# Two queued steps of the second query group, and one copy, are put at other places in the start-up order of a fused attention and feed-forward kernel

## The chip, the core and the metric

The kernel runs on one core of a Trainium2 chip. The time is device microseconds for one launch; a lower time is better. The core has a matrix engine (TensorE, PE in the profile), three others that compute on tiles (VectorE = DVE, ScalarE = ACT, GpSimd = POOL) and a queue engine (SyncE = SP). Each engine works through its own list of instructions in order, and waits on semaphores for the others. PE's weight loads have a row of their own, PEld.

## The reference

Inputs are q, k and v of shape 4 x 4 x 1088 x 32 (batch, heads, rows, head dimension), two sketches S1 and S2 of 8 x 32, and two weight matrices, w_in (128 x 2048) and w_out (2048 x 128). What is computed:

```
phi(x)[i*8+j] = (S1 x)[i] * (S2 x)[j]           for q and for k: 64 features
kv  = sum over rows of phi(k) v^T               64 x 32 per head
z   = sum over rows of phi(k)                   64 per head
att = (phi(q) kv) / (phi(q) z + 1e-6)           32 per row and head
x   = att, the four heads side by side          4352 x 128
h   = x w_in ;  g = h - tanh(h) ;  out = g w_out
```

## The kernel before, in words

The 4352 rows of x are cut into 11 groups of columns (`GROUPS`); group 0 has 256 columns, group 1 has 448, group 2 has 384. For each group g the work goes through these steps, named by the tags in the code:

- `qT{g}` (L643, DVE): the queries, loaded from memory into `qraw`, are transposed into `qT`. For batch 0 the queries come in three loads: group 0's 8 blocks, group 1's 14 blocks, and the rest.
- `p{g}` (L665, PE): the projections of the queries by the sketches, into two banks of `ps`. Those of group 1 lie in banks 4 and 5.
- `qq{g}` (L694, DVE) transposes them back, `au{g}` (L697, DVE) and `dn{g}` (L700, DVE) make the parts of the denominator, `ds{g}` (L710, PE, for groups 0, 1 and 4) adds the two halves, `rd{g}` (L723, DVE) takes the reciprocal, `an{g}` (L727, DVE) scales by it.
- `qp{g}` (L739, one half on POOL, one on DVE for groups 0 and 1) forms the products, `qpT{g}` (L746, DVE) transposes them. `qpT01` is the second half of group 0's.
- `w{g}` (L681, PE) multiplies by the sums of the keys (`ndw`); `x{g}` copies the result to `xT` in bf16. For group 0 there are two copies: `x0` on ACT and `x0b` on DVE (both L755).
- `h{g}_{jb}` (L845, PE) is one 128-row tile of x w_in, `t{g}_{jb}` (L848, ACT) its tanh, and L858 (PE) the product with w_out, 16 tiles to a group. h uses three banks in turn, so h tile n waits for the tanh of tile n - 3.

The tanh part is subtracted from a linear part, x (w_in w_out), whose matrix is multiplied out once in the kernel (L783, L788, L797).

The keys of a batch come first: `kT00` and `kT01` (L549, DVE) transpose the two loads of batch 0, `kp00` and `kp01` (L556, PE) project them, `kab0` (L567, DVE) transposes the projections back, `gram0` (L593, PE), `gm0` (L600, DVE), `fold0` (L605, PE) and `u0` (L608, DVE) fold them into weights of the queries' projections, and `wk00`, `wk02` on DVE and `wk04`, `wk06`, `wk08` on POOL (L582) form the key features. `sums00` and `sums01` (L621, PE) sum them against v, `kvz0` (L629, ACT), `turn0` (L632, PE) and `ndw0` (L635, ACT) turn these sums for use by `w{g}`. After `ndw0`, ACT casts the first half of w_in (`cin0`, `cin1`, L768) and then does its half of x's first copy (`x0`). POOL casts w_out in three pieces (`cout0`, `cout4`, `cout8`, L772) and the second half of w_in (`cin2`, `cin3`, L768).

The loads of batch 0 and of the weights are issued at the start, nearly all on ACT's queue: both parts of k, the first two of q, two of v, w_in and w_out in halves with the rest of q between. Two more parts of v are issued on SP (L446). The load of batch 1's keys (`lk1`, L438 on SP) is made to wait for `qpT01`, and v and q of batch 1 are queued behind it.

The order of instructions on each engine comes from a list scheduler (`Program.schedule`) with its own costs, run on the host when the kernel is built; `Program.line(tags)` adds an order between neighbours of a list of tags. Such an order is no semaphore wait: if both steps are on one engine, the second is simply put behind the first in that engine's list, and across engines it shapes only the plan. PE also gets filler products of zeros (`warm`, L495, and `warm_more`, L501 and L506) wherever the plan has room.

Of the kernel before, what the change touches and what calls it, by code (L numbers as in the profile page):

```python
# [317 lines left out]
def bass_polysketch_attn__then__act_tanh_shrink_kernel(nc, q, k, v, S1, S2, moe_w_in, moe_w_out, out):  # L318
    P = Program(nc)

    def sb(name, shape, dtype=F32):
        return nc.alloc_sbuf_tensor(name, shape, dtype).ap()
# [21 lines left out]
    s2m = sb("s2m", [128, H, D])  # L344
    wkm = sb("wkm", [128, 2, R, 2])
# [572 lines left out]
    for g in range(NG):  # L918
# [37 lines left out]
        if g > 1:  # L956
# [1 line left out]
    P.tags["wk08"].deps.add(P.tags["au0"])  # L958
    P.tags["cout4"].deps.add(P.tags["au1"])
    P.tags["lk1"].deps.add(P.tags["qpT01"])  # L960
    P.line(["kT00", "wkm", "kT01", "qT0", "qT1", "kab0", "kps0", "s2m", "gm0", "wk00", "u0", "wk02", "qq0", "au0", "dn0", "qq1",
            "rd0", "an0_1", "an0_0", "qp00", "qpT00", "qpT01", "au1", "dn1", "x0b",
            "rd1", "an1_1", "an1_0", "qp10", "qpT10", "qpT11", "qT2", "x1", "qq2", "au2", "dn2", "ds2", "dt2", "rd2", "an2", "kT10", "kT11", "qpT21", "qpT20", "qT3"])
    for g in range(4, NG):
        P.line([f"x{g - 2}", f"qT{g}"])
# [2 lines left out]
        P.line([f"wk{b}0", f"u{b}", f"wk{b}2"])  # L968
    P.line(["x1", "kT10"])
    P.line(["wk10", "u1", "wk12"])  # L970
    P.line(["pS", "kp00", "kp01", "pSel", "gram0", "fold0", "p0", "p1", "sums00", "ds0", "sums01", "turn0", "w0"])
    P.line(["w0", "h0_2", "ds1", "w1", "p2"])
    P.line(["kvz0", "ndw0", "cin0", "cin1", "x0", "t0_0"])
    P.line(["wk04", "wk06", "wk08", "qp01", "cout0", "cout4", "cin2", "qp11", "cin3", "cout8"])
# [29 lines left out]
```

## Time and profile before

| | |
|---|---|
| Median of 3 runs | 106.52 us (105.25 to 107.47) |
| The profiled execution's own time | 104.81 us |
| Its span in the trace | 102.9 us |
| Busy share: PE, ACT, DVE, POOL | 94%, 76%, 73%, 32% |
| Chain that ended last, by engine | PE 79%, ACT 10%, DMA 4%, DVE 2% |

The profiled execution is one launch; its own time is 1.91 us longer than its span, and the rest of the text adds nothing to that difference. In the rows, the first number is the start in us from the span's start and the second the duration; `x16` is the number of instructions merged into a row, and what stands in brackets is the idle time before it and what ended that.

### The profile page before, as it was taken

How to read it: one execution, taken by the hardware profiler on the slowest of the kernel's cores; microseconds unless marked ns; L12 is line 12 of the kernel's file. 1: busy time of each engine (PE TensorE's matmuls, PEld its weight loads, DVE VectorE, ACT ScalarE, POOL GpSimd, SP SyncE). 2: the span in 40 equal slices, each digit the busy share in tenths (PEclk: the TensorE clock that was granted, in tenths of full speed). 3: DMA queues.
4: the chain of work that ended last, by engine and by line, in shares of the span. 5: the costliest groups of instructions: out<-in, count | busy, mean ns of one | idle time of the engine just before them, and what ended most of it. 6: DMA issues, size and time to landing. Idle time of an engine off the chain costs nothing.

```text
span 102.9 us, 3124 instructions
## 1 busy us (share of the span) xinstructions
PE 96.9 (94%) x1254; PEld 49.6 (48%) x1257; DVE 74.7 (73%) x211; ACT 78.3 (76%) x190; POOL 33.2 (32%) x61
## 2 busy tenths in 40 slices
PE   5978999999999999999999999999999999999970
PEld 4424634633757454456345443544735554445660
DVE  3559969799869999799659999779937989440220
ACT  0013189798994987976979999897697998999950
POOL 5548477223740602871200300584300020400000
PEclk9999999999999999999999999999999999999999
DMA  2999999810299144015898032002401402205043
GB/s 49 303 277 288 370 263 301 246 35 0 43 312 272 38 71 70 3 25 78 274 252 195 4 49 34 0 0 38 69 2 24 69 0 41 42 3 89 0 63 71
DMA packets 23679, 11.22 MB, mean 109 GB/s; under 512 B 17648, under 2 KB 22384, under 8 KB 23664
## 3 DMA queue, kind: packets, MB, share of 16 engines
q1 hardware_dynamic: 20000, 7.38, 32.1%
q10 hardware_dynamic: 3664, 3.64, 11.9%
q8 instruction: 10, 0.16, 0.7%
q14 instruction: 5, 0.04, 0.1%
HBM read 8.78 MB, written 2.23 MB: 107 GB/s over the span
## 4 chain that ended last, share of the span: by engine, by line
PE 79%; ACT 10%; DMA 4%; DVE 2%; ACTq 1%; issue 1%
PE ps L845 29%; PE ps L858 24%; ACT tt L848 8%; PE ps L621 5%; DMA qraw<-in_q_dram 4%; PE ps L681 4%; PE ps L665 4%; PE ps L837 3%; PE ps L877 2%; PE ps L556 2%; PE ps L593 1%; ACT w_in L768 1%; PE ps L797 1%; PE ps L495 1%; PE ps L783 1%; PE ps L605 1%
## 5 line engine op out<-in xcount | busy, mean ns | idle before, releaser
L848 ACT ACTIVATE tt<-ps 128x448 bf16<-128x448 f32 (+3 forms) x176 | 72.7, 537 | 6.7 <-PE ps L845 6.2
L845 PE MATMUL ps<-xT,w_in 128*128 128x448 bf16 (+3 forms) x174 | 54.8, 333 | 0.5 <-ACT tt L848 0.2
L858 PE MATMUL ps<-tt,w_out 128*128 128x448 bf16 (+3 forms) x159 | 49.0, 336 | 0.1
L845 PEld LDWEIGHTS ps<-xT,w_in 128*128 128x128 bf16 x176 | 16.3, 97 | 25.4 <-ACT tt L848 17.5
L739 POOL TENSOR_TENSOR qp<-an,qq 128x384 f32<-128x384 f32 (+3 forms) x15 | 12.7, 846 | 35.5 <-DVE an L727 34.9
L858 PEld LDWEIGHTS ps<-tt,w_out 128*128 128x128 bf16 x160 | 15.8, 99 | 6.9
L582 POOL TENSOR_TENSOR wk<-kab 128x256 f32<-128x256 f32 (+1 forms) x18 | 12.1, 674 | 17.1 <-DVE kab L567 15.5
L866 DVE STREAM_TRANSPOSE osb<-ps 128x448 f32<-128x448 f32 (+2 forms) x9 | 5.6, 619 | 11.0 <-PE ps L858 6.7
L746 DVE STREAM_TRANSPOSE qpT<-qp 128x448 f32<-128x448 f32 (+3 forms) x22 | 11.9, 571 | 1.4 <-POOL qp L739 1.0
L495 PE MATMUL ps<-wz 128*128 128x256 bf16 (+1 forms) x25 | 6.4, 388 | 1.1 <-DVE hmask L472 1.1
L694 DVE STREAM_TRANSPOSE qq<-ps 128x448 f32<-128x448 f32 (+3 forms) x11 | 6.4, 586 | 1.2 <-PE ps L665 1.1
L643 DVE STREAM_TRANSPOSE qT<-qraw 128x256 f32<-128x256 f32 (+2 forms) x12 | 6.4, 530 | 1.2 <-DMA qraw<-in_q_dram 1.2
L629 ACT ACT_TABLE_LOAD x1 | 1.3, 1283 | 7.3 <-issue 7.3
L760 DVE CAST xT<-ps 128x448 bf16<-128x448 f32 (+3 forms) x10 | 6.0, 600 | 0.7 <-PE ps L681 0.5
L549 DVE STREAM_TRANSPOSE kT<-kraw 128x576 f32<-128x576 f32 (+1 forms) x8 | 5.5, 722 | 1.2 <-DMA kraw<-in_k_dram 1.2
L716 DVE COPY ps<-dn 32x24 f32<-32x24 f32 (+3 forms) x32 | 5.9, 184 | 0.6
L681 PE MATMUL ps<-qpT,ndw 64*32 64x224 f32 (+3 forms) x176 | 6.2, 337 | 0.1
L629 ACT COPY kvz<-ps 128x128 f32<-128x128 f32 x4 | 1.1, 265 | 6.4 <-PE ps L621 6.4
L665 PE MATMUL ps<-qT,wq 64*32 64x224 f32 (+3 forms) x176 | 5.9, 333 | 0.0
L582 DVE TENSOR_TENSOR wk<-kab,ps 128x512 f32<-128x512 f32 x8 | 5.4, 678 | 0.0
L621 PE MATMUL ps<-wk,vx 128*32 128x64 f32 x288 | 5.1, 221 | 0.0
L621 PEld LDWEIGHTS ps<-wk,vx 128*32 128x32 f32 x288 | 4.2, 110 | 1.4 <-issue 1.1
(86 smaller groups left out, 83.6 us busy)
## 6 DMA issues: line engine op xcount, KB each, us to landing
kraw<-in_k_dram SPq DMA_DIRECT2D x3, 544.0 KB, 5.6
qraw<-in_q_dram SPq DMA_DIRECT2D x3, 544.0 KB, 6.0
vx<-in_v_dram SPq DMA_DIRECT2D x10, 144.0 KB, 4.5
w_in_f<-in_moe_w_in_dram ACTq DMA_DIRECT2D x2, 512.0 KB, 8.0
w_out_f<-in_moe_w_out_dram ACTq DMA_DIRECT2D x2, 512.0 KB, 9.3
out_dram<-osb SPq DMA_DIRECT2D x16, 56.0 KB, 1.9
out_dram<-osb SPq DMA_DIRECT2D x16, 48.0 KB, 1.9
vx<-in_v_dram SPq DMA_DIRECT2D x4, 112.0 KB, 5.2
```

The costliest lines, as they stand in the source:

```text
L495: P.op("tensor", 213 if x < 12 else 290, lambda e, n=1 if x < 16 else 2: e.matmul(ps[:, 3, 0:256 * n], wz[:, 0:128], wz[:, None, :].to_bro ...
L582: P.op(eng, 60 + 64 * n if eng == "vector" else pool(64 * n), lambda e: e.tensor_tensor(out=wk[:, t0:t1, :, :].rearrange("p t h (i j) -> p ...
L621: ins = e.matmul(ps[32 * h:32 * h + 32, sbk, 0:64], vx[i][:, h, t, :], wk[:, t, h, :], start=(t == 0), stop=(t == 8), tile_position=(0, 32 ...
L643: P.op("vector", dve(hi - lo), lambda e, i=b % 2, lo=lo, hi=hi: e.transpose(out=qT[i][:, lo:hi], in_=qraw[i][:, lo:hi]), r=[("qraw", b % 2 ...
L665: ins = e.matmul(o, wq[64 * r:64 * r + 64, b, y, :, :].rearrange("p h x -> p (h x)"), src, start=True, stop=True, tile_position=(64 * r, 3 ...
L681: ins = e.matmul(ps[32 * h:32 * h + 32, 2 + u, 0:32 * nh], ndw[i][64 * u:64 * u + 64, 32 * h:32 * h + 32], src[64 * u:64 * u + 64, h // 2, ...
L694: P.op("vector", dve(16 * n), lambda e: e.transpose(out=a[:, 0:n, :].rearrange("p (r m) x -> p r (m x)", r=2), in_=ps[:, pb[0]:pb[1] + 1:p ...
L739: P.op("vector" if dv else "gpsimd", 95 + 33.2 * m if dv else pool(32 * m), lambda e, lo=lo, dv=dv: e.tensor_tensor(out=qp[u][:, lo:lo + m ...
L746: P.op("vector", dve(32 * m), lambda e, lo=lo: e.transpose(out=qpT[u][:, 32 * lo:32 * (lo + m)], in_=qp[u][:, lo:lo + m, :].rearrange("p n ...
L845: P.op("tensor", pe(n), lambda e, jb=jb, bk=bk: e.matmul(bk[:, 0:n], w_in[:, 128 * jb:128 * jb + 128], xT[:, t0:t0 + n], start=True, stop= ...
L848: P.op("scalar", act(n), lambda e, ts=ts, bk=bk: e.activation(out=tt[:, ts, 0:n], in_=bk[:, 0:n], func=AF.Tanh, scale=-1.0), r=[kb], w=[(" ...
L858: P.op("tensor", pe(n), lambda e, jb=jb, ts=ts: e.matmul(acc[:, 0:n], w_out[:, jb, :], tt[:, ts, 0:n], start=(jb == 0 and g < 2), stop=(jb ...
```

## The change

Only the lists given to `Program.line` differ; no instruction is added, removed or resized. Four things move:

- `qT1` no longer stands between `qT0` and `kab0`, but between `dn0` and `rd0`.
- `qq1` no longer stands between `dn0` and `rd0`, but behind `qpT01`.
- `x0b` comes ahead of `au1` and `dn1`, and behind `qq1`.
- `p1` no longer stands between `p0` and `sums00`, but between `sums01` and `turn0`.

```
-    P.line(["kT00", "wkm", "kT01", "qT0", "qT1", "kab0", "kps0", "s2m", "gm0", "wk00", "u0", "wk02", "qq0", "au0", "dn0", "qq1",
-            "rd0", "an0_1", "an0_0", "qp00", "qpT00", "qpT01", "au1", "dn1", "x0b",
+    P.line(["kT00", "wkm", "kT01", "qT0", "kab0", "kps0", "s2m", "gm0", "wk00", "u0", "wk02", "qq0", "au0", "dn0", "qT1",
+            "rd0", "an0_1", "an0_0", "qp00", "qpT00", "qpT01", "qq1", "x0b", "au1", "dn1",
...
-    P.line(["pS", "kp00", "kp01", "pSel", "gram0", "fold0", "p0", "p1", "sums00", "ds0", "sums01", "turn0", "w0"])
+    P.line(["pS", "kp00", "kp01", "pSel", "gram0", "fold0", "p0", "sums00", "ds0", "sums01", "p1", "turn0", "w0"])
```

In the lists that result, ACT, POOL and SP have the same instructions in the same order as before. DVE's list differs by the steps named, and from `rd1` on it is the same. On PE, `p1` moves, and the scheduler also deals out what lies around it anew: one filler product of 512 columns (L495) fewer ahead of `gram0`, one more between `sums00` and `ds0`, none between `sums01` and `turn0`; one more filler (L506) ahead of `ds1`; `w1` and `p2` stand behind 14 instead of 13 tiles of group 0's h; and up to the linear part's turns (L783) the tiles of group 1's h and the products of groups 0 and 1 alternate in another pattern. From there on PE's list is the same.

## The prediction

> **What bounds the kernel now.** I read the table of stages first, then the chain that ended last, and then the first 20 us in order of time.
>
> ```profile
> 20.00:30.00 10.00, 9.86 (x120) 4.64 (x119) 8.24 (x23) 9.49 (x21) 4.82 (x7) 1.00 0.29 93
> ```
>
> The stage row gives the length and then the busy time of PE, PEld, DVE, ACT and POOL. From 20 us on PE is busy 9.86 of 10 us, and ACT 9.49. There is no slack in which a late start could be made good, and none in which an early one is lost: what the start-up gains or loses by 20 us, the end should gain or lose. Later loads wait for copies of x, so they move along. The question is the start-up, and there the chain reads:
>
> ```profile
> 2.14 4.53 DMA qraw<-in_q_dram
> ...
> 8.06 0.38 PE ps L593 x18
> ...
> 9.57 0.78 PE ps L665 x32
> 10.35 0.81 PE ps L621 x48
> 11.16 0.34 PE ps L710 x2
> ...
> 11.72 0.52 PE ps L621 x24
> ...
> 12.58 0.34 PE ps L632
> ...
> 13.21 1.03 ACT w_in L768 x2
> 14.25 0.17 ACT xT L755
> ...
> 14.47 0.50 PE ps L845 x3
> ```
>
> The chain starts with a load of queries, the second group's. It lands at 2.14 + 4.53 = 6.67 us, qT1 transposes it, and only behind qT1 does DVE turn to kab0, on which the keys' whole work hangs. From the keys' sums it goes through kvz, turn, ndw, two casts of w_in and ACT's half of the first x to the first h tiles at 14.47. The second group's queries are on this path only because of their place in DVE's list.
>
> **The change part by part.** First the stall that goes.
>
> ```profile
> 4.65 1.30 PE L556 MATMUL ps<-kT,wkm 64*32 64x288 f32 x16
> 5.14 0.40 DVE L643 STREAM_TRANSPOSE qT<-qraw 128x256 f32<-128x256 f32 x1
> 6.70 0.65 DVE L643 STREAM_TRANSPOSE qT<-qraw 128x448 f32<-128x448 f32 x1 [1.16 <-DMA qraw<-in_q_dram]
> 7.26 0.74 DVE L567 STREAM_TRANSPOSE kab<-ps 128x576 f32<-128x576 f32 x1
> 11.54 0.27 DVE L723 RECIPROCAL ps<-ps 128x16 f32<-128x16 f32 x1
> ```
>
> What kab0 reads is ready when the projections end, 4.65 + 1.30 = 5.95, and DVE is free of qT0 at 5.54. Where DVE waits for PE it starts 0.04 us behind it (ds0 ends at 11.50, the reciprocal starts at 11.54). So kab0 can start at 5.99 instead of 7.26: **1.27 us earlier**. The lower bound is the idle time itself, 1.16; the upper counts kab0 from the end of qT1, 7.35 - 5.99 = 1.36.
>
> Next, whether the rest follows. sums00 has a load of its own to wait for:
>
> ```profile
> 3.12 0.45 ACTq L446 DMA_DIRECT2D vx<-in_v_dram  x1
> vx<-in_v_dram ACTq DMA_DIRECT2D x1, 144.0 KB, 5.7
> ```
>
> The last piece of v lands at 3.12 + 5.7 = 8.82; loads don't move. p0 is 128 of the 352 columns of p0 and p1 and would end at about 9.57 + 0.28 - 1.27 = 8.58; sums00 is no longer behind p1, so it waits for v, starts at 8.86 and ends at 9.67. ds0 behind it is due at 11.16 - 1.27 = 9.89. The wait is new, and 0.22 us of slack covers it: **0**. Each us by which v comes later than about 9.04 costs one.
>
> qT1 takes the place of qq1 between dn0 and rd0:
>
> ```profile
> 10.96 0.64 DVE L694 STREAM_TRANSPOSE qq<-ps 128x448 f32<-128x448 f32 x1
> 12.63 0.77 DVE L746 STREAM_TRANSPOSE qpT<-qp 128x256 f32<-128x256 f32 x2
> 13.45 0.45 PE L681 MATMUL ps<-qpT,ndw 64*32 64x128 f32 x16
> 13.32 0.28 DVE L697 TENSOR_TENSOR au<-qq 128x112 f32<-128x112 f32 x1
> 13.63 0.30 DVE L700 TENSOR_REDUCE dn<-au 128x28 f32<-128x140 f32 x1
> 15.15 0.34 DVE L723 RECIPROCAL ps<-ps 128x28 f32<-128x28 f32 x1 [0.85 <-PE ps L710]
> ```
>
> 0.65 against 0.64 us, and in both cases it hides the time that PE needs for ds0: **0**. Its load, landed at 6.67, is long there.
>
> p1 goes between sums01 and turn0, on the path. Before, sums01 ended at 12.24 and turn0 waited until 12.58 for kvz; now p1 fills that gap and runs over. Alone on PE a product of p1's shape (w1, quoted further down) takes 0.54, which ends it at 12.78 on the old clock: 0.20 late. Bounds: in the chain p0 and p1 share 0.78; by columns (224 of 352) p1's part is 0.50, and if turn0 overlaps it further the loss goes to nothing; if its start costs as much as a wait, 0.25. I take the upper middle, **+0.20**, since the w1 row is the nearest. The way to the first h tiles then shifts by 1.27 - 0.20 = **1.07**, to 13.40.
>
> qq1 and x0b behind qpT01: qpT01 ends at 13.40 - 1.27 = 12.13, qq1 adds 0.64, x0b follows at 12.77 (w0 ends at 13.90 - 1.27 = 12.63) and takes until about 13.06. ACT's half ends at 14.42 - 1.07 = 13.35, so qq1 lies beside ACT's casts: **0**, with 0.29 of cover; beyond it x0b sets the first h. au1 and dn1 take 0.61 (13.32 to 13.93) and end at 13.67. PE comes to ds1 behind three h tiles, at 14.97 - 1.07 = 13.90, and one more filler of 256 columns, 0.11. So PE waits for nothing; had dn1 come later than 14.0, PE would stand still there with h3 and all behind it, and then ACT. rd1 starts at 15.15 - 1.07 + 0.11 = 14.19: the second group's chain is **0.96** earlier.
>
> ```profile
> 18.00 0.54 PE ps L681 x16
> 18.65 0.62 DVE L760 CAST xT<-ps 128x448 bf16<-128x448 f32 x1 [0.46 <-PE ps L681]
> 19.12 0.94 ACT L848 ACTIVATE tt<-ps 128x256 bf16<-128x256 f32 x3 [0.62 <-PE ps L845]
> ```
>
> w1 now stands behind one more h tile. At ACT's pace of 0.31 a tile (0.94 for three) it starts at 18.00 + 0.31 - 1.07 = 17.24, and x1 ends at 19.27 - 0.76 = 18.51. ACT's 0.62 of waiting behind w1 and p2 stays as it is. Behind it ACT has two tanh tiles (from 18.36 to 18.98) instead of three before the first tile of group 1, which PE can have ready about 19.05 (x1's end, two products and the tile itself): a gap of **+0.1**. Of the loads, k, v and q of batch 1 are issued 1.27 earlier, behind qpT01; that is the last of the rivals, and here 0.
>
> The sum: -1.27 + 0.20 + 0 + 0.11 on the second group alone (the one more tile covers it) + 0.1 = **-0.95**, bounds -0.75 to -1.2. The profiled execution would go from 104.81 to 103.86. It was 1.71 below the median of the runs, 106.52; on that scale the forecast is 105.57, **105.6 us**.
>
> **A slow clock** would be a rival of its own.
>
> ```profile
> 1.05 2.74 PE L495 MATMUL ps<-wz 128*128 128x256 bf16 x12 [1.05 <-DVE hmask L472]
> 8.97 0.60 PE L495 MATMUL ps<-wz 128*128 128x512 bf16 x2
> ```
>
> At the start twelve fillers of 256 columns take 0.23 us each; at 8.97 two of 512 take 0.60, which is 0.15 for 256. So PE becomes faster somewhere between. If the slow part reached past 7 us, the gram products, moved from 8.06 to about 6.8, and the one behind them would run at the slow pace: 0.38 x 0.23 / 0.15 is 0.2 more, some 0.3 with the second, and the time 105.9. For it speaks that before nothing on the path ran on PE between 7.0 and 8.0; against it, that the pace at 8.97 is already the fast one. The Trainium skill (TensorE: Matmul & The Clock Gate, Part 1) says that PE runs at half clock until a busy window of about 3.4 us has passed, and that these windows run free of the kernel's start. By that rule the full clock could come as late as 7.9 us, an estimate from that page, which would be this case; the one trace can't tell how far the moment wanders.
>
> **The rivals.** *The stall is longer in the usual run.* If all of the 1.71 us by which the median lies above the profile were a later landing of this one load, the gain would be 0.95 + 1.71 = 2.66 and the time 103.9. For it: most of the input comes in the first 20 us, and this is the one load on the chain. Against: v is queued right behind it on ACT; were v as late, sums00 would start at 10.57 and ds0 be 1.49 late, leaving about 105.3. *The wait moves to v.* If v lands 0.75 us later than in this trace, beyond its slack by 0.53, 106.1 is left. The slack of 0.22 speaks for it, the common queue against it. *No stall in the usual run.* If the load mostly lands before 5.5 us, nothing is removed and p1's 0.20 and the 0.1 are left: 106.8. The profiled run, faster than all three others, makes that unlikely.
>
> *Slower: the last piece of w_out.*
>
> ```profile
> 6.30 0.93 ACTq L462 DMA_DIRECT2D w_out_f<-in_moe_w_out_dram  x1
> w_out_f<-in_moe_w_out_dram ACTq DMA_DIRECT2D x1, 512.0 KB, 10.3
> 13.42 0.35 SPq L438 DMA_DIRECT2D kraw<-in_k_dram  x1
> 17.58 1.04 POOL L772 CAST w_out<-w_out_f 128x1024 bf16<-128x1024 f32 x1
> 16.00:18.00 2.00, 2.00 (x23) 0.88 (x27) 1.97 (x4) 2.00 (x9) 1.80 (x3) 1.00 1.00 299
> ```
>
> It lands at 16.6, is cast by POOL in 1.04, and PE's list asks for it about 18.5. So it decides from a landing at 17.4, and from there PE stands still us for us, with group 1's tiles behind the product. Batch 1's loads now start 1.27 earlier, while the DMA engines are full (share 1.00, 299 GB/s). If the 544 KB of k went wholly ahead of it, 1.82 us, it would land at 18.4 and the gain be gone (106.6); with v's 544 KB as well, at 20.2, a stall of 2.8 and 108.4; a little of q on top passes 2%. The Trainium skill (DMA: Bandwidth & Descriptors, Queues, rings and completion order) has each engine take turns between queues packet by packet; by that rule k gets half of the 1.27 us, an estimate of 0.64, and the piece lands before 17.4. No run shows the shares.
>
> **How the numbers follow.** Forecast 0.46, slow clock 0.04, longer stall 0.27, wait on v 0.09, no stall 0.05, w_out 0.09. A difference under 2%, 2.13 us, is about what a measurement of this kernel can't tell from none. The likeliest case has its own range of 104.6 to 106.6, from the bounds of the sum and the spread of the three runs. Faster by over 2% (below 104.39) is most of the longer stall (0.23) and the lower tail of the forecast (0.08): 0.31. Slower by over 2% (above 108.65) is the worse half of the w_out case with the runs' spread: 0.07. The rest, 0.62, is within 2%. The range from 103.7 to 107.0 takes in the long stall's end and the milder part of the slower cases.
>
> **What would show it.** kab0 at about 6.0 us, no DVE idle before qT1, sums00 at about 8.9 behind v, turn0 right behind p1, the first h tiles near 13.4, rd1 near 14.2, tiles of group 1 near 18.7, and the span about 101.9. It is wrong if kab0 starts early and the first h tiles do not, if PE idles before ds1 or before a product behind the cast of w_out, or if the first 20 us come out 1 us shorter and the span doesn't.

## The result, and the profile after

The changed kernel takes 104.62 us (median of 21 runs, 103.95 to 105.93); the kernel before, run beside it, 105.34 us (21 runs, 104.68 to 107.47). The ratio is **0.9946, 95% interval 0.9922 to 0.9971**: faster by about 0.6 us, well under 2%. Two more measurements of the same program gave 0.9922 (0.9889 to 0.9955) and 0.9938 (0.9894 to 0.9981). Executions more than 1.5% above the fastest of their kernel (8 of these 21 before, 4 of the 21 after) are in the medians and not in the ratios. The profiled execution took 104.31 us, with a span of 102.5.

The chain that ended last, in the changed kernel (start, duration, what):

```profile
1.66 4.08 DMA qraw<-in_q_dram
5.76 0.45 DVE qT L643
6.21 0.68 DVE kab L567
6.93 0.38 PE ps L593 x18
...
9.48 0.88 PE ps L621 x48
10.36 0.32 PE ps L495
10.81 0.23 PE ps L495
11.04 0.47 PE ps L621 x24
11.51 0.54 PE ps L665 x16
12.05 0.27 PE ps L632
...
13.87 0.50 PE ps L845 x3
```

kab0 stands at 6.13 instead of 7.26 (by the timeline), and what leads up to it is the first group's load of queries, not the second's. p1 (L665) is on the chain, between sums01 and turn0. The first h tiles come at 13.87 instead of 14.47. So 1.13 us were won at kab0 and 0.60 are left at the first h tiles. The rows of the timeline show where the rest went:

```profile
6.13 0.74 DVE L567 STREAM_TRANSPOSE kab<-ps 128x576 f32<-128x576 f32 x1
9.45 0.74 PEld L621 LDWEIGHTS ps<-wk,vx 128*32 128x32 f32 x48 [0.89 <-DMA vx<-in_v_dram]
10.85 0.27 DVE L723 RECIPROCAL ps<-ps 128x16 f32<-128x16 f32 x1 [0.39 <-PE ps L710]
14.66 0.34 DVE L723 RECIPROCAL ps<-ps 128x28 f32<-128x28 f32 x1 [0.54 <-PE ps L710]
17.39 1.04 POOL L772 CAST w_out<-w_out_f 128x1024 bf16<-128x1024 f32 x1 [0.40 <-DMA w_out_f<-in_moe_w_out_dram]
```

sums00 now waits for v and starts 3.35 us behind kab0, where 2.87 were forecast (8.86 - 5.99); the first reciprocal, which before had no idle time ahead of it, waits 0.39 for ds0. Further on, POOL's last cast of w_out waits for its load. From 20 us on, PE is as busy as before:

```profile
20.00:30.00 10.00, 9.93 (x126) 4.92 (x125) 8.40 (x23) 9.33 (x20) 4.82 (x7) 1.00 0.30 88
```

### The profile page after: what moved, and what is told of

The parts are those of the page before. It is cut to its first block, busy times and chain, and to the rows that moved or that the text cites. A ratio compares the mean times of both kernels' runs of the same rounds, so it can differ in the third digit from the quotient of the medians.

```text
span 102.5 us, 3128 instructions
## 1 busy us (share of the span) xinstructions
PE 96.7 (94%) x1256; PEld 49.8 (49%) x1259; DVE 74.8 (73%) x211; ACT 78.4 (76%) x190; POOL 33.2 (32%) x61
## 3 DMA queue, kind: packets, MB, share of 16 engines
HBM read 8.78 MB, written 2.23 MB: 107 GB/s over the span
## 4 chain that ended last, share of the span: by engine, by line
PE 80%; ACT 9%; DMA 4%; DVE 2%; ACTq 1%; issue 1%
PE ps L845 29%; PE ps L858 24%; ACT tt L848 8%; PE ps L621 5%; PE ps L681 4%; PE ps L665 4%; DMA qraw<-in_q_dram 4%; PE ps L837 3%; PE ps L877 2%; PE ps L556 2%; PE ps L593 1%; PE ps L495 1%; ACT w_in L768 1%; PE ps L783 1%; PE ps L797 1%; PE ps L605 1%
## 5 line engine op out<-in xcount | busy, mean ns | idle before, releaser
L495 PE MATMUL ps<-wz 128*128 128x256 bf16 (+1 forms) x24 | 6.1, 383 | 1.1 <-DVE hmask L472 1.1
L665 PE MATMUL ps<-qT,wq 64*32 64x224 f32 (+3 forms) x176 | 6.1, 334 | 0.0
```

Of the source, the lines that this page charges most:

```text
L495: P.op("tensor", 213 if x < 12 else 290, lambda e, n=1 if x < 16 else 2: e.matmul(ps[:, 3, 0:256 * n], wz[:, 0:128], wz[:, None, :].to_bro ...
L665: ins = e.matmul(o, wq[64 * r:64 * r + 64, b, y, :, :].rearrange("p h x -> p (h x)"), src, start=True, stop=True, tile_position=(64 * r, 3 ...
```

## The experiments

My theory after the result was V: the new wait for v eats part of the saved stall. Its rivals were P (p1 ahead of turn0 eats it) and L (the loads of this one execution were late by chance). Every kernel here is the changed kernel with one or two edits. The milestones in their traces, in us, with the first reciprocal as rd0:

| kernel | kab0 | sums00 | sums00 - kab0 | rd0 - kab0 | first h | span |
|---|---|---|---|---|---|---|
| before | 7.26 | 10.28 | 3.02 | 4.28 | 14.47 | 102.9 |
| changed | 6.13 | 9.48 | 3.35 | 4.72 | 13.87 | 102.5 |
| again | 5.90 | 8.78 | 2.88 | 4.30 | 13.22 | 101.9 |
| again_b | 5.85 | 8.95 | 3.10 | 4.47 | 13.34 | 102.1 |
| stall_back | 7.69 | 10.53 | 2.84 | 4.27 | 14.97 | 103.5 |
| no_fill | 5.93 | 8.93 | 3.00 | 4.30 | 13.34 | 101.8 |
| p1_late | 6.38 | 9.28 | 2.90 | 4.31 | 13.85 | 102.6 |
| v_first | 6.00 | 8.92 | 2.92 | 4.32 | 13.33 | 105.4 |
| k1_early | 6.08 | 9.57 | 3.49 | 4.85 | 13.95 | 108.9 |
| k1_hold2 | 6.42 | 9.78 | 3.36 | 4.73 | 14.16 | 102.7 |
| wout_first | 6.25 | 9.31 | 3.06 | 4.43 | 13.94 | 102.9 |
| v_hold | 6.26 | 9.10 | 2.84 | 4.26 | 13.54 | 102.1 |
| v_hold_no_fill | 6.32 | 9.17 | 2.85 | 4.31 | 13.74 | 102.2 |
| v_hold_b | 6.55 | 9.44 | 2.89 | 4.30 | 13.87 | 102.5 |

**The same program again** (no edit).

> The changed kernel once more, for a second trace of the same program beside the others. Theory V (the saved stall is partly eaten by a new wait for v, ahead of sums00): 0.5 us (0.5%) faster than before; sums00 starts on PE later than its other inputs allow (about 8.9 us) by 0.3 to 0.7 us, and kab0 starts near 6.1. Rival P (p1 ahead of turn0 eats the gain): the same time, but sums00 starts by 9.0 and turn0 is the step that is late. Rival L (the loads of this one execution were late by chance): kab0 starts near 6.0, sums00 near 8.9 and the span is shorter than 102.5 us by 0.3 or more.

> The changed kernel beside the guarded one on the same chip, for a direct comparison. 0.5 to 0.8% under before, as in its two earlier measurements; kab0 near 6 us; the first h tiles between 13.2 and 13.9, by how late v lands.

The ratios stand above. Of again, from the chain and the timeline:

```profile
5.90 0.79 DVE kab L567
...
8.78 0.88 PE ps L621 x48
...
10.86 0.54 PE ps L665 x16
11.40 0.27 PE ps L632
...
13.22 0.50 PE ps L845 x3
```

```profile
17.09 1.04 POOL L772 CAST w_out<-w_out_f 128x1024 bf16<-128x1024 f32 x1 [0.75 <-DMA w_out_f<-in_moe_w_out_dram]
```

Here sums00 doesn't wait, and the first h tiles and the span come out as the prediction had them (13.4, 101.9). So L holds for the single trace: over the three traces of this one program kab0 moves between 5.85 and 6.13 and sums00 between 8.78 and 9.48, as the loads land. The wait for v is there in some executions, 0 to 0.5 us long.

**The stall put back.**

```
-            "qT0", "kab0", ... "dn0", "qT1", "rd0"
+            "qT0", "qT1", "kab0", ... "dn0", "rd0"
```

> The changed kernel with qT1 back between qT0 and kab0, all else as changed: it takes away the one part that is held to bring the gain. If the gain is the stall: kab0 back at about 7.3 us, no wait for v, and the time at or up to 0.3 us above the kernel before (p1 ahead of turn0 left alone, 0.1 to 0.2). If the other moves bring part of it: under the kernel before by 0.2 us or more.

Measured 1.0037 (1.0002 to 1.0072) of the kernel before.

```profile
7.12 0.65 DVE L643 STREAM_TRANSPOSE qT<-qraw 128x448 f32<-128x448 f32 x1 [1.61 <-DMA qraw<-in_q_dram]
7.69 0.74 DVE L567 STREAM_TRANSPOSE kab<-ps 128x576 f32<-128x576 f32 x1
```

The whole gain is the stall: with it back, the kernel is no faster than before. The other moves, left alone, cost some 0.4 us (0.0 to 0.8 by the interval). Of that the trace shows 0.07 up to the first h tiles (7.28 behind kab0, 7.21 before) and 0.1 behind them (88.53 against 88.43 to the end of the span); the rest isn't placed. The stall itself is 1.61 here and 1.16 in the first trace, so its length also goes with the load.

**v ahead of the second queries.**

```
-    load_q(0, -2982, ..., tag="lq1")
-    load_v(0, -2980, ("scalar", "scalar", "sync", "sync"), [("qsum",)])
+    load_v(0, -2982, ("scalar", "scalar", "sync", "sync"), [("qsum",)])
+    load_q(0, -2980, ..., tag="lq1")
```

> The changed kernel, with the two loads of v on ACT's queue issued ahead of the second group's queries. Theory V: v lands about 0.5 us earlier, sums00 starts at 8.8 to 9.0, rd0 at about 10.4 instead of 10.85, the first h tiles near 13.5 instead of 13.87, and the time is 0.3 to 0.5 us under the changed kernel, about 0.9% under before. Rival P: sums00 earlier, the end not; within 0.1 us of the changed kernel.

Measured 0.9982 (0.9937 to 1.0027): no gain that can be told. sums00 did follow kab0 by 2.92 us, as expected. But the last half of w_out landed 12.70 us after its issue, and PE stood still for it. The profiled execution, at 107.21 us, is the longest of the kernel's, so this trace shows that the wait can happen, not how much it is worth. It moved the question to that load. v ahead of the queries, by itself, doesn't bring the missing part of the gain.

**No filler behind sums00.** The edit orders the filler products from the 21st on behind ds0.

```
+    [x.order.add(P.tags["ds0"]) for x in [y for y in P.ops if y.prio == 5000][20:]]
```

> The changed kernel without the one filler product of 512 columns that the scheduler put between sums00 and ds0. Theory V: once sums00 is late, the filler stands on the path, so ds0 and rd0 come up to 0.21 us (512 columns at PE's fast pace) earlier, rd0 at about 10.65, and the time is 0.1 to 0.2 us under the changed kernel. Rival P: no difference.

Inconclusive in time: 0.9987 (0.9937 to 1.0037). The trace shows the small thing: sums00 0.13 us late against the 2.87 forecast, and rd0 still on time, 4.30 behind kab0. In again_b, with the filler, 0.23 us late make rd0 0.17 late against again. That is one pair of traces.

**p1 behind turn0.**

```
-    "sums00", "ds0", "sums01", "p1", "turn0", "w0"
+    "sums00", "ds0", "sums01", "turn0", "p1", "w0"
```

> The changed kernel with p1 put behind turn0 instead of ahead of it. Theory V: turn0 follows kvz at once, 0.1 to 0.2 us earlier, so ndw0, the casts and the first h tiles are 0.1 to 0.2 earlier; qq1 and x0b are later by up to 0.3 but have that cover; the time is 0 to 0.15 us under the changed kernel. Rival P: the time is 0.3 us or more under the changed kernel.

0.9953 (0.9923 to 0.9983), like the changed kernel. In the trace, turn0 starts 5.36 us behind kab0, against 5.43 in again and 5.32 in the kernel before. So p1's place costs 0.1. It isn't won back: p1 now stands ahead of w0 in PE's list, and the first h tiles start 7.47 us behind kab0 instead of 7.32. ACT's half of x is ready at 13.68, x0b at 13.70, and two filler products (L501) hold PE until 13.74 by the chain; the trace doesn't tell which of them the first h tiles waited for:

```profile
13.24 0.50 PE L501 MATMUL ps<-wz 128*128 128x384 bf16 x2
13.41 0.29 DVE L755 CAST xT<-ps 128x128 bf16<-128x128 f32 x1
13.85 0.49 PE L845 MATMUL ps<-xT,w_in 128*128 128x256 bf16 x3
```

P falls: turn0 is 0.1 late by p1, less than the 0.20 that the forecast already holds, and the time is the changed kernel's.

The trace shows something else. kab0 comes at 6.38 here, though the keys were transposed as early as in again. It waits for the keys' projections (L556), which start at 4.71 in both; each takes 684 ns here, and 402 to 427 in again:

```profile
4.71 1.61 PE L556 MATMUL ps<-kT,wkm 64*32 64x288 f32 x16
6.38 0.78 DVE L567 STREAM_TRANSPOSE kab<-ps 128x576 f32<-128x576 f32 x1 [0.98 <-PE ps L556]
```

**The last half of w_out.** The new theory W: batch 1's loads, released earlier, push this load back until PE waits behind its cast. The rival N: its landing differs by chance. Larger and smaller contention, by what releases batch 1's keys:

```
-    P.tags["lk1"].deps.add(P.tags["qpT01"])
+    P.tags["lk1"].deps.add(P.tags["au0"])     # k1_early;   k1_hold2: P.tags["rd1"]
```

> The changed kernel with the load of batch 1's keys released by au0 (about 9.6 us) instead of by the second half of qpT0 (about 12.1): the suspected contention made larger. Theory W (batch 1's loads push back the last half of w_out, whose cast PE then waits for): w_out lands 1 to 2 us later, at 18.5 us or later, POOL's last cast waits for it, PE stands still before a product, and the time is 1 to 3 us above the changed kernel. Rival N (the DMA engines serve the older loads first, the landing differs by chance): w_out lands at 17 to 17.6 as in the changed kernel, and the time is within 0.3 us of it.

Measured 1.0557 (1.0495 to 1.0619), with all four runs between 110.15 and 111.32 us. The chain, PE's wait, the timeline and the stages:

```profile
6.50 15.00 DMA w_out_f<-in_moe_w_out_dram
21.51 0.05 issue
21.56 1.05 POOL w_out L772
22.61 0.05 issue
22.66 0.40 PE ps L858
```

```profile
PE ps L858 <- POOL w_out L772: 3.7, 1, 3.7
```

```profile
9.66 0.35 SPq L438 DMA_DIRECT2D kraw<-in_k_dram  x1
21.56 1.04 POOL L772 CAST w_out<-w_out_f 128x1024 bf16<-128x1024 f32 x1 [4.49 <-DMA w_out_f<-in_moe_w_out_dram]
```

```profile
20.50:21.00 0.50, 0.00 (x0) 0.00 (x0) 0.41 (x3) 0.00 (x0) 0.00 (x0) 1.00 0.32 86
21.50:24.00 2.50, 1.34 (x6) 0.88 (x7) 0.00 (x0) 0.32 (x1) 1.04 (x1) 0.50 0.01 3
26.00:28.00 2.00, 2.00 (x7) 0.61 (x5) 1.82 (x6) 1.60 (x4) 0.55 (x1) 0.50 0.00 0
28.50:29.00 0.50, 0.50 (x4) 0.29 (x3) 0.50 (x2) 0.50 (x2) 0.50 (x1) 1.00 0.00 0
```

Keys issued 3.07 us earlier (9.66 against 12.73) make w_out land at 21.5 instead of 17.3. That is 4.2 us, more than the 1.8 that the keys' 544 KB take at the 299 GB/s of the prediction's row; v and q of batch 1 are queued behind them, and how much each takes isn't shown. PE stands still for 3.7 us, and the stage rows' clock (the 1.00 or 0.50 ahead of the DMA share) is at half until 28.2, which makes it 6 us and not 4. So W holds for a large head start. My expectation of 1 to 3 us was too small by the landing, 1 to 2 us later expected and 4.2 measured, and by the clock.

> The changed kernel with the load of batch 1's keys released by rd1 (about 14.1 us) instead of by the second half of qpT0 (about 12.1). Theory W: w_out lands at 16.6 or before, POOL's last cast doesn't wait, and the time is 0.2 to 0.4 us under the changed kernel; 1.0% or more under before. Rival N: no difference, or slower, if batch 1's keys then come too late for kT10 at about 21.5.

Measured 0.9944 (0.9912 to 0.9977): no better than the changed kernel. In its trace the keys are issued at 15.32, the cast waits only 0.23 and starts at 17.52, but v is late again (sums00 3.36 behind kab0). w_out itself landed at 17.5 (6.29 + 11.2), where 16.6 or before was expected, later than in any trace of the changed kernel (16.8 to 17.3) although the keys were held back. So at the size of the change N isn't refuted: the landing scatters by more than the hold brings. One guard alone shows nothing.

```
-    load_q(0, -2955, groups[0][1] + groups[1][1], CB, "scalar")
-    load_w_out(1, -2950)
+    load_w_out(1, -2955)
+    load_q(0, -2950, groups[0][1] + groups[1][1], CB, "scalar")
```

> The changed kernel with the last half of w_out issued ahead of the last part of batch 0's queries on ACT's queue. Theory W: w_out lands about 1 us earlier, near 16.3, its cast doesn't wait, the queries land near 15.5 for qT2 at about 16.6, and the time is 0.2 to 0.4 us under the changed kernel. Rival N: within 0.1 us of it.

Measured 1.0005 (0.9968 to 1.0043): the gain is gone. The cast doesn't wait (17.18), but the issue of the queries, now last in ACT's queue, blocks ACT:

```profile
6.45 3.96 ACTq L453 DMA_DIRECT2D qraw<-in_q_dram  x1
10.44 1.28 ACT L629 ACT_TABLE_LOAD   x1 [10.44 <-issue]
11.74 0.27 ACT L629 COPY kvz<-ps 128x128 f32<-128x128 f32 x1
```

ACT issues for 3.96 us, loads its table until 11.72, and kvz, on the path, is held up; turn0 then waits 0.18 for it. The first h tiles start 7.69 us behind kab0 instead of 7.32, so this is some 0.4 us of the loss; the rest isn't placed.

**Both loads guarded**: v ahead of the second queries, and batch 1's keys released by rd1.

> The changed kernel with v's two loads ahead of the second group's queries on ACT's queue, and with the load of batch 1's keys released by rd1: both late loads guarded at once. If the two waits (on v, on the last half of w_out) are what the change still loses: sums00 at 8.8 to 9.2 whatever kab0 does, the last cast of w_out by 17.2 without PE standing still, the span near 101.9 us and the time 0.2 to 0.4 us under the changed kernel, 0.8 to 1.0% under before. If the loads only change places among themselves: the time within 0.2 us of the changed kernel.

> The same, without the filler product between sums00 and ds0. If sums00 is in time, the filler lies in PE's slack and the time is the same within 0.1 us; if sums00 is still late, up to 0.2 us less.

> The guarded kernel again, v ahead and batch 1's keys held. If the guards bring something of their own: 0.3 to 0.5% under the changed kernel run beside it, about 1.1% under before. If its first measurement was chance: within 0.2% of the changed kernel.

Measured 0.9884 (0.9851 to 0.9917), without the filler 0.9881 (0.9851 to 0.9910), and again 0.9906 (0.9877 to 0.9935), with the changed kernel at 0.9938 beside the last. The medians, 103.97, 104.05 and 104.15 us, lie under those of the changed kernel (104.41 to 104.62). Of v_hold:

```profile
9.10 0.88 PE L621 MATMUL ps<-wk,vx 128*32 128x64 f32 x48
16.80 1.04 POOL L772 CAST w_out<-w_out_f 128x1024 bf16<-128x1024 f32 x1
```

In all three traces sums00 follows kab0 by 2.84 to 2.89 us, and the cast has no wait ahead of it. Of the first, a part is owed to kab0, which comes late there, at 6.26 to 6.55, and so leaves v more time. The filler makes no difference to the time once v is in time. The intervals of the last pair overlap, so the 0.3% between guarded and changed isn't settled by that pair alone; but all three guarded ratios (0.9881 to 0.9906) lie below all three of the changed kernel (0.9922 to 0.9946), so a gain from the guards is likely. What the hold brings of it isn't shown: w_out lands at 16.6 to 16.9 here, and at 16.6 and 16.7 in p1_late and no_fill, which don't have it.

## Why the prediction came out as it did

The direction and the mechanism were right; the size was off: -0.95 us forecast, -0.57 measured in the first comparison (105 x 0.0054), -0.82 and -0.65 in the two others. The time lay in the range, but that says little: the range was 3.3 us wide, and the forecast of 105.6 was 1 us too high because it started from 106.52, the median of three runs, where 21 runs give 105.34.

- *The stall, -1.27.* Right in the main. kab0 stands at 5.85 to 6.55 in every trace with qT1 moved, 6.17 in the mean; 5.99 was forecast. Two things that the forecast took as fixed lead to it: the first queries' load, where it lands late (in the changed kernel's trace qT0 waits 0.62 for it), and the pace of the keys' projections.
- *sums00 behind v, "0.22 us of slack covers it: 0".* This step failed: a term put at nothing measured 0.27 us in the mean. The slack wasn't there: sums00's end at 9.67 and ds0's due time of 9.89 have the filler of 512 columns between them, which I had listed in the change and left out of this step. 512 columns are 0.21 us of PE (one filler takes 0.39, two 0.60). And v's landing, 8.82 in the first trace, moves between 8.2 and 9.5: over the eight traces with qT1 moved and v behind the queries, three of them of the changed kernel, sums00 is 0 to 0.62 us behind the forecast spacing, 0.27 in the mean. rd0 shows it nearly in full: 4.72 behind kab0 in the changed kernel's trace, 4.30 in again. This fits the missing part of the gain, 0.13 to 0.38 us, and the guarded kernels make it likely; v alone put ahead didn't show it. Two smaller terms of the step were off too. p0, taken as 0.28 by its share of columns, lasts 0.45 (8.19 to 8.64 in again); so the agreement of again with the 2.87 is partly luck, since sums00 stands there behind p0, not v. And from v's landing to sums00 it is about 0.2 us, not 0.04 (3.1 + 6.1 against 9.45 in the changed kernel's trace). The rival "the wait moves to v", to which I gave 0.09, was a part of the likeliest case.
- *qT1 beside ds0, 0.* Right: no DVE idle ahead of rd0 wherever v is in time (10.20 in again).
- *p1 ahead of turn0, +0.20.* Half: turn0 stands 5.43 behind kab0 in again, 5.32 before, so 0.11. p1 itself took the 0.54 that w1's row gave (10.86 to 11.40).
- *qq1 and x0b, 0; ds1, 0.11 on the second group.* Right: in again x0b ends at 12.97 and ACT's copy at 13.18; PE finds dn1 ready.
- *w1, +0.1.* Near in size, but not at this place: from the first h tiles to the end of the span it is 88.43 before, 88.63 in the changed kernel and 88.68 in again, so 0.2. Group 1's first tile, at 19.65 before, still comes 0.65 and 1.23 earlier (19.00 and 18.42), as much as the first h tiles; the projections of batch 1's keys, at 23.93 before, come only 0.45 and 1.04 earlier (23.48 and 22.89). The 0.2 is lost between them, where the order of tiles and products differs; the cause stays open.
- *A slow clock.* Not at the gram products: their row is 0.38 or 0.39 in every trace. But the slow pace does reach the keys' projections in p1_late and v_hold_b, and kab0 is some 0.5 us later there (6.38 and 6.55) than in again. Before the change this would have lain under the wait for the queries.
- *A longer stall in the usual run, or none.* Both traces with qT1 ahead of kab0 have it, 1.16 and 1.61 (stall_back). The high median was three runs' chance.
- *Slower by the last piece of w_out.* The place and the cause were right, as k1_early shows; the price wasn't: us for us from 17.4, a landing at 21.5 would cost 4.1 us, and it cost 6, by the clock. The changed kernel doesn't come to it: the load lands at 17.3, 17.1 and 16.8 in its three traces, and PE loses 0.2 at most (again). That wait in again also shows that it decides somewhat before the 17.4 that I gave. The rule of the Trainium skill (DMA: Bandwidth & Descriptors, Queues, rings and completion order), that queues take turns, is neither shown nor excluded by these runs: in the five traces with the keys issued 0.69 to 1.33 us earlier than before and no other load moved, w_out landed 0 to 0.7 later, with no order by the head start. It doesn't give the 4.2 us of k1_early by itself either, since the whole head start was 3.07.

## What to carry to other kernels

When a step is moved off a load that it waits for, the next load in line can become the bound, and its slack must be counted with everything that stands between, fillers too. One trace gives one draw of the landing times, and of PE's pace at the start; a wait that is 0 in it can be half a us in the next, so a slack under that is no cover. A load released much earlier takes its bandwidth from what is still under way: guard the oldest load that the critical engine will ask for, and move a load in an issuing engine's queue only after looking at what that engine has to do next.

## What the runs showed of the hardware

Three things I had not expected. In two traces a PE that stood still for 2 us or more paid for it a second time. In the profiled execution of v_first:

```profile
18.30:20.40 2.10, 0.03 (x1) 0.00 (x0) 1.87 (x8) 0.61 (x2) 1.04 (x1) 1.00 0.97 227
20.40:21.50 1.10, 1.08 (x8) 0.77 (x9) 0.00 (x0) 0.47 (x2) 0.00 (x0) 1.00 0.39 135
22.00:25.00 3.00, 3.00 (x10) 1.14 (x9) 2.25 (x6) 2.51 (x7) 0.89 (x2) 0.50 0.03 12
25.50:28.00 2.50, 2.50 (x35) 0.91 (x39) 2.08 (x4) 2.10 (x5) 0.33 (x2) 1.00 0.00 0
```

PE is idle from 18.3 to 20.4 and then busy; more than 1 us later the clock goes to half for about 3.4 us (21.7 to 25.1), though PE is busy all through. In k1_early, with 3.7 us of idling, it is about 6.8 us (21.4 to 28.2), twice that. No shorter standstill was tried.

Issuing a load is not always short: the same issue that takes 0.75 us in one place of ACT's queue (before) takes 3.96 in another (wout_first).

And the moment at which PE's slow pace at the start ends differs from execution to execution: the keys' projections from 4.7 us on take 402 to 427 ns each in again, and 684 ns each in p1_late (to 6.3 us) and v_hold_b (to 6.5 us). The stage rows' clock shows 1.00 there all the same, so only the instructions tell it.
